# One decode step of cached attention with a token mixer: the query projection laid out by shifted slices of x, and the place of the last output-weight load

## The chip, the core and the metric

The kernel runs on one core of one Trainium2 chip. A core has five engines that run side by side: TensorE (PE, matrix multiplications; its weight loads are shown as PEld), VectorE (DVE), ScalarE (ACT), GpSimd (POOL) and SyncE (SP). Here SP issues all large transfers from main memory (HBM) into on-chip memory (SBUF, 128 partitions), on one queue that 16 DMA engines work through. Matrix products land in PSUM, in banks of 128 partitions x 512 fp32. The metric is the device time of one execution in microseconds (us), as the median of several executions.

## What is computed

One token attends over a cache of 65536 positions with 16 query heads and 8 key/value heads (two query heads share one of them), head size 256. Beside it a small token-mixing MLP works on the same x, and a gate mixes the two. The reference, cut:

```python
B, Sq, D = 1, 1, 448
Hq, Hkv, Sk, Dh = 16, 8, 65536, 256
...
q = (x @ wq).reshape(B, Sq, Hq, Dh).transpose(0, 2, 1, 3)
k = jnp.repeat(k_cache, rep, axis=1)
v = jnp.repeat(v_cache, rep, axis=1)
scores = jnp.einsum("bhqd,bhkd->bhqk", q, k) * (Dh ** -0.5)
p = _softmax(scores, axis=-1)
o = jnp.einsum("bhqk,bhkd->bhqd", p, v)
a = o.transpose(0, 2, 1, 3).reshape(B, Sq, Hq * Dh) @ wo
...
h = _layernorm(x)
u = _gelu(jnp.einsum("bsd,sf->bdf", h, w1) + b1)
b = (jnp.einsum("bdf,fs->bds", u, w2) + b2).transpose(0, 2, 1)
...
g = _sigmoid((x * gate_w).sum(-1, keepdims=True))
return g * a + (1 - g) * b
```

Everything is bf16. The K and V caches are 268 MB each, wq and wo 3.7 MB each.

## The kernel before

Engines are ordered by semaphores written out by hand; no scheduler moves anything. In the setup a small recorder, `do` (lines 41 to 91), adds the waits that follow from the names of what each step reads and writes. Afterwards semaphores are waited on one by one (`take` waits for a semaphore and takes the count off again).

**Chunks.** Each of the 8 KV heads is cut into 6 chunks (`SIZES`, two of 6 and four of 5 blocks of 16 x 128 positions), 48 chunks in all. K of a chunk goes to `kbuf[i % 2]` and V to the single `vbuf`; both hold 6.3 MB. Per chunk:

- DVE (`turns`, L559) turns each K block in 32x32 blocks of fp32 pairs into one of three `kT` tiles.
- PE (`scores`, L685) multiplies `kT` with the window `qw`, which holds the current head pair's queries, into the PSUM bank `sc`. ACT (L632) takes the exponential into `p_t`, DVE turns it (L605), and PE (`p_v`, L699) multiplies it with V of that chunk into `pv`, one chunk later.
- DVE adds `pv` to `og` (`drain_pv`, L569 and L570) and raises `s_vf`: `vbuf` is free.

At the end of a head, DVE forms the next head's window (`queries`, L504), PE turns `og` upright (`o_turn`, L709), DVE divides (`heads`, L577, after `take(dve, s_wo, 16)`), and four matmuls with that head pair's output weights `wo` (L755) add to `acc` and raise `s_oo`: `wo` is free.

**SP's order.** wq (into `vbuf`, which V 0 needs later), K 0, K 1; then SP waits for the projection; V 0, `wo` 0, K 2; then for each i V i (`load_v`, waits for `s_vf` at i + 1), at the second chunk of a head the head's `wo` (`load_wo`, waits for `s_oo`), and K i + 2 (`load_k`). The last V goes in four pieces into the free `kbuf[0]` (L534). The last head's `wo` is issued behind them in two halves with semaphores of their own (L535 to L542).

**The projection** (`project`, L436). x is 448 long. `turn_x` lays it out in columns of 128 partitions (`xT`, 5 columns: three of 128 values, and two for the last 64 values, spread over even and odd partitions). For each of 8 head pairs n, four matmuls (x as the stationary side with one column, 512 columns of wq as the moving side) give one row of 512 values, on partition 32a of `sc` (n = 0 to 3) or `pv` (n = 4 to 7), with `tile_position` choosing column group a. DVE copies both banks (L457), PE turns the rows upright with 32 matmuls of one column (`turn_q`, L466), DVE copies (`qT`, L480), PE spreads `qT` to blocks of 32 partitions with 16 matmuls against an identity (`spread`, L488), DVE copies the result to `qr` (L498). `queries` (L504) multiplies columns of `qr` with a block mask into `qw`.

**The tail** (L762 to L853). With the last V pieces landing, PE multiplies piece by piece (`upright`, L795, then `turned`, L806), DVE divides (L577), PE multiplies with the two halves of `wo` (L840, each half behind its own wait), DVE copies `acc4` to `res` (L847), and SP stores it. POOL waits for the store.

```python
        sp.wait_ge(s_oo, HKV - 1)
        s_wl = [nc.alloc_semaphore(f"s_wl{r}") for r in range(2)]
        for r in range(2):
            at = (HKV - 1) * 512 + r * DH
            sp.dma_start(
                out=wo[:, r, :, :].rearrange("p c n -> p (c n)"),
                in_=A_wo[at:at + DH, :].rearrange("(p c) n -> p (c n)", c=2),
            ).then_inc(s_wl[r], 16)
```

Of the kernel before, what the change touches and what calls it, by code (L numbers as in the profile page):

```python
# [9 lines left out]
BF16 = mybir.dt.bfloat16  # L10
# [4 lines left out]
HQ = 16  # L15
# [79 lines left out]
def kernel(  # L95
# [49 lines left out]
    zb = const.tile([1, 2], FP32, name="zb")  # L145
    ident = const.tile([128, 128], BF16, name="ident")
    block = const.tile([128, 4], FP32, name="block")
# [7 lines left out]
    xd = const.tile([1, 2, 128], BF16, name="xd")  # L155
    xT = const.tile([128, KA + 2], BF16, name="xT")
    xg = const.tile([1, D], FP32, name="xg")
# [11 lines left out]
    h_bc = const.tile([128, D], FP32, name="h_bc")  # L169
    qT = const.tile([128, 2, HQ], BF16, name="qT")  # L170
    qr = const.tile([128, 8, HQ], BF16, name="qr")
    qw = const.tile([128, 8, WIN], BF16, name="qw")
# [8 lines left out]
    tick = const.tile([1, 1], FP32, name="tick")  # L181
    q_row = const.tile([128, 2, 512], BF16, name="q_row")
    oT = const.tile([128, 4], BF16, name="oT")
# [24 lines left out]
    def critical():  # L208
# [55 lines left out]
        for k, src in enumerate((B_w1[0, :], B_b1, B_w2[:, 0])):  # L264
# [7 lines left out]
                out=ident[:], in_=ident[:], compare_op=ALU.not_equal, fill=1.0, base=0,  # L272
                pattern=[[-1, 128]], channel_multiplier=1,
            ), reads=["ident"], writes=["ident"],
# [8 lines left out]
        for t, key, val in (  # L283
            (one_b, "one_b", 1.0), (xd, "xd", 0.0), (one_f, "one_f", 1.0), (zero_b, "zero_b", 0.0),
            (pat, "pat", 0.0), (qw, "qw", 0.0), (col_f, "col_f", 1.0), (pv, "pv", 0.0), (sc, "sc", 0.0),
        ):
            do("dve", lambda e: e.memset(t[:], val), writes=[key])
# [23 lines left out]
        do("pe", turn_x, reads=["x_row", "xd", "one_b"], writes=["x_ps"])  # L311
        do("dve", lambda e: e.tensor_copy(out=xT[:], in_=x_ps), reads=["x_ps"], writes=["xT"])

# [86 lines left out]
        def turn_w(e):  # L400
            for k in range(3):
                last = e.matmul(
                    w_ps[:, k * NF:(k + 1) * NF], lhsT=wrow[:, k, :], rhs=ident[0:NF, 0:NF],
                    start=(k == 0), stop=(k == 2), skip_group_check=True,
                )
            return last
# [26 lines left out]

        q_rows = (sc, pv)

        def project(e):  # L436
            for n in range(8):
                half, a = divmod(n, 4)
                dst = q_rows[half][32 * a:32 * a + 1, :]
                for k in range(KA):  # L440
                    e.matmul(
                        dst, lhsT=xT[:, k:k + 1], rhs=wqa[:, k, n * 512:(n + 1) * 512],
                        start=(k == 0), stop=False, tile_position=(0, 32 * a),
                    )
                last = e.matmul(
                    dst, lhsT=xT[:, KA + half:KA + half + 1], rhs=wqb[:, a * 512:(a + 1) * 512],
                    start=False, stop=True, tile_position=(0, 32 * a),
                )
            return last

        do("pe", project, reads=["wqa", "wqb", "xT", "pv", "sc"], writes=["q_rows"])
        do.need("sp", writes=["wqa", "wqb"])
        load_v(0)
        load_wo(0)
        for half in range(2):
            do(
                "dve", lambda e: e.tensor_copy(out=q_row[0:97, half, :], in_=q_rows[half][0:97, :]),  # L457
                reads=["q_rows"], writes=[f"q_row{half}"],
            )
        q_ps = misc[:, 448:448 + 2 * HQ]  # L460

        def turn_q(e, a):
            for h in (2 * a, 2 * a + 1, 2 * a + 8, 2 * a + 9):
                src = q_row[32 * a:32 * a + 1, h // 8, h % 2 * DH:(h % 2 + 1) * DH]
                for c in range(2):
                    last = e.matmul(  # L466
                        q_ps[:, c * HQ + h:c * HQ + h + 1], lhsT=src[:, c::2],
                        rhs=one_b[32 * a:32 * a + 1, 0:1], start=(h == 0 and c == 0),
                        stop=(h == HQ - 1 and c == 1), tile_position=(32 * a, 0),
                        skip_group_check=True,  # L470
                    )
            return last

        for a in range(4):
            do(
                "pe", lambda e: turn_q(e, a), reads=["q_row0", "q_row1", "one_b", "x_ps"],
                writes=["q_ps", "x_ps"],
            )
        do(
            "dve", lambda e: e.tensor_copy(out=qT[:].rearrange("p c h -> p (c h)"), in_=q_ps),  # L480
            reads=["q_ps"], writes=["qT"],
        )
        qr_ps = misc[:, 0:8 * HQ]

        def spread(e):
            for b in range(4):
                for a in range(4):
                    last = e.matmul(  # L488
                        qr_ps[32 * a:32 * a + 32, b * 2 * HQ:(b + 1) * 2 * HQ],
                        lhsT=ident[:, 32 * b:32 * b + 32], rhs=qT[:].rearrange("p c h -> p (c h)"),  # L490
                        start=(b == 0), stop=(b == 3), tile_position=(0, 32 * a),
                        skip_group_check=True,
                    )
            return last

        do("pe", spread, reads=["ident", "qT", "q_ps"], writes=["qr_ps", "q_ps"])
        do(
            "dve", lambda e: e.tensor_copy(out=qr[:].rearrange("p b h -> p (b h)"), in_=qr_ps),  # L498
            reads=["qr_ps"], writes=["qr"],
        )  # L500

        def queries(h, r):
            cols = slice(PAD + 16 * r, PAD + 16 * r + 97, 32)
            return dve.tensor_tensor(  # L504
                out=qw[:, :, cols], in0=qr[:, :, bass.ds(h, 1)].to_broadcast([128, 8, 4]),
                in1=block[:].rearrange("p (o a) -> p o a", o=1).to_broadcast([128, 8, 4]),
                op=ALU.mult,
            )

        for r in range(2):  # L510
            do("dve", lambda e: queries(r, r), reads=["qr", "block"], writes=["qw"])
        do(
# [7 lines left out]
        for i in range(1, total - 1):  # L520
            load_v(i)
            if i % PER == 1 and PER < i < total - PER:
                load_wo(i // PER)
            if i + 2 < total:
                load_k(i + 2)
# [6 lines left out]
        for k in range(len(edges) - 1):  # L532
            lo, hi = edges[k] * DH, edges[k + 1] * DH
            sp.dma_start(out=vlast[:, lo:hi], in_=src[:, lo:hi]).then_inc(s_last[k], 16)  # L534
        sp.wait_ge(s_oo, HKV - 1)  # L535
        s_wl = [nc.alloc_semaphore(f"s_wl{r}") for r in range(2)]
        for r in range(2):
            at = (HKV - 1) * 512 + r * DH
            sp.dma_start(
                out=wo[:, r, :, :].rearrange("p c n -> p (c n)"),  # L540
                in_=A_wo[at:at + DH, :].rearrange("(p c) n -> p (c n)", c=2),
            ).then_inc(s_wl[r], 16)  # L542

# [47 lines left out]
        def dve_chunk(i, head):  # L591
# [14 lines left out]
            if c == PER - 1 and i < total - 1:  # L606
                for r in range(2):
                    queries(head + r, r)
                den_rows()
                dve.tensor_scalar(  # L610
                    out=og[:], in0=og[:], scalar1=dsum[:, 0:1], scalar2=None, op0=ALU.add
                ).then_inc(s_d, 1)
# [8 lines left out]
        with nc.Fori(0, HKV - 1, 1, engines=[DVE], head_slot={DVE: 0}) as turn_v:  # L621
            for i in range(1, PER + 1):
                dve_chunk(i, turn_v * 2 + 2)
        for i in range(total - PER + 1, total):
# [92 lines left out]

        do.need("pe", reads=["qw", "pv", "mask", "acc", "xb_ps", "w_ps", "qr_ps"])
        do.need("pe", writes=["qr_ps", "w_ps", "xb_ps"])
        c_reg = pe.alloc_register("c_reg")  # L720
# [109 lines left out]
        pe.wait_ge(s_last[3], 16)  # L830
        turned(edges[3], edges[4]).then_inc(s_fp, 1)
        dve.wait_ge(s_fp, 4)
        heads().then_inc(s_fd, 1)
        pe.wait_ge(s_fd, 4)
        for k in range(4):
            r, cc = divmod(k, 2)
            if cc == 0:
                pe.wait_ge(s_wl[r], 16)
            for a in range(4):
                ins = pe.matmul(  # L840
                    acc4[32 * a:32 * a + 1, 0:DQ], lhsT=oT[:, 2 * cc + r:2 * cc + r + 1],
                    rhs=wo[:, r, cc, DQ * a:DQ * (a + 1)], start=False, stop=(k == 3),
                    tile_position=(0, 32 * a), skip_group_check=True,
                )
# [7 lines left out]
        ).then_inc(s_out, 16)  # L852
        pool.wait_ge(s_out, 16)  # L853

# [32 lines left out]
```

## Time and profile before

| what | value |
|---|---|
| runs shown | 1266.63, 1266.64, 1266.64, 1267.09 us |
| median of them | 1266.64 us |
| the profiled execution, its own time | 1266.44 us |
| its span (first to last recorded work) | 1264.7 us |
| mean granted TensorE clock | 0.79 of full |
| read from HBM | 544.22 MB, 430 GB/s over the span |

The profile is of one execution. Busy times are sums over the span; a group of instructions is one source line on one engine, with its count and the mean duration of one. Of the groups, these touch the change (line, work, count, total busy us, mean ns):

```profile
L685 PE MATMUL sc<-kT,qw 128*128 128x512 bf16 x2048 | 565.3, 438 | 454.9 <-PEq L681 454.9
L605 DVE STREAM_TRANSPOSE pT<-p_t 128x512 bf16<-128x512 bf16 x48 | 34.2, 712 | 117.6 <-DVEq L551 117.6
L755 PE MATMUL acc<-wo,oT 128*1 128x448 bf16 x28 | 7.5, 399 | 12.7 <-PEq L752 12.7
```

Behind the second bar stands the idle time of the engine just before such work, and what ended most of it (PEq and DVEq are the engines' own sequencers, which wait for semaphores). An arrow `out<-in` names tiles, and `x` a count. The table of transfers gives for each kind the bytes of one and the median time from issue to landing, which includes the time behind other transfers in the queue.

### The profile page before, as it was taken

To read this page: it belongs to the slowest core of one execution; us is meant where nothing else is said; L and a number is where in the kernel's file an instruction comes from. 1 tells how busy PE (TensorE), PEld (TensorE's weight loads), DVE (VectorE), ACT (ScalarE), POOL (GpSimd) and SP (SyncE) were. 2 spreads that over 40 slices of the span, in tenths; PEclk is the share of its full clock that TensorE was granted. 3 is DMA by queue.
4 is the path that set the end of the run, shared out by engine and by line. 5 is a ranking of instruction groups with operands and counts; after the bars stand their busy time and mean duration, and the time that the engine had idled before them with its cause. 6 is when DMAs were issued, how large, how long until landed. Compare 5 with 4: busy or idle time off the path is not lost. (4 is left out here: it accounts for less than half of the span.)

```text
span 1264.7 us, 10796 instructions
## 1 busy us (share of the span) xinstructions
PE 720.3 (57%) x4344; PEld 282.1 (22%) x4344; DVE 665.5 (53%) x473; ACT 50.1 (4%) x127; POOL 76.7 (6%) x98
## 2 busy tenths in 40 slices
PE   2845656466554655556555565555645665467546
PEld 1311222122211222222222221222212222122212
DVE  4745554465544645455545554465445644466444
ACT  0000000000000000000000000000000000000000
POOL 0001010110110101101111011000000000000000
PEclk9887877868887787777877778778877778777887
DMA  9999999999999999999999999999999999999998
GB/s 411 418 439 429 438 438 425 438 434 429 438 438 427 429 443 427 438 434 433 437 433 427 432 431 443 435 432 431 434 430 439 433 424 435 441 429 439 433 430 343
DMA packets 16844, 544.35 MB, mean 430 GB/s; under 512 B 1856, under 2 KB 3906, under 8 KB 4162
## 3 DMA queue, kind: packets, MB, share of 16 engines
q1 hardware_dynamic: 16744, 544.22, 99.6%
q8 instruction: 4, 0.07, 0.0%
q14 instruction: 6, 0.05, 0.0%
q10 hardware_dynamic: 90, 0.01, 0.0%
HBM read 544.22 MB, written 0.00 MB: 430 GB/s over the span
## 5 line engine op out<-in xcount | busy, mean ns | idle before, releaser
L685 PE MATMUL sc<-kT,qw 128*128 128x512 bf16 x2048 | 565.3, 438 | 454.9 <-PEq L681 454.9
L559 DVE STREAM_TRANSPOSE kT<-kbuf 128x2048 f32<-128x2048 f32 x256 | 571.4, 2284 | 308.2 <-DVEq L551 307.8
L685 PEld LDWEIGHTS sc<-kT,qw 128*128 128x128 bf16 x2048 | 213.9, 108 | 805.5 <-issue 642.6
L699 PE MATMUL pv<-vbuf,pT 128*4 128x512 bf16 x2008 | 132.0, 416 | 56.3 <-PEq L733 55.8
L605 DVE STREAM_TRANSPOSE pT<-p_t 128x512 bf16<-128x512 bf16 x48 | 34.2, 712 | 117.6 <-DVEq L551 117.6
L570 DVE TENSOR_TENSOR og<-pv,og 128x512 f32<-128x512 f32 x39 | 27.0, 692 | 111.5 <-DVEq L551 109.7
L699 PEld LDWEIGHTS pv<-vbuf,pT 128*4 128x4 bf16 x2008 | 51.2, 92 | 134.8 <-issue 96.0
L632 ACT ACTIVATE p_t<-sc 128x512 bf16<-128x512 f32 x48 | 28.7, 597 | 1191.3 <-PE sc L685 1191.3
L659 POOL TENSOR_SCALAR t_b<-t_b 128x448 f32<-128x448 f32 x14 | 7.9, 564 | 358.2 <-ACT t_b L641 358.2
L663 POOL TENSOR_SCALAR t_b<-t_b,hw 128x448 f32<-128x448 f32 x14 | 8.9, 638 | 335.1 <-ACT t_b L649 335.1
L569 DVE COPY og<-pv 128x512 f32<-128x512 f32 x8 | 5.5, 692 | 37.7 <-DVEq L551 37.7
L668 POOL TENSOR_TENSOR ymix<-ymix,t_b 128x448 f32<-128x448 f32 x14 | 16.1, 1148 | 1.1
L667 POOL TENSOR_TENSOR t_b<-t_b,u_b 128x448 f32<-128x448 f32 x14 | 15.8, 1127 | 1.2
L662 POOL TENSOR_TENSOR t_b<-t_b,u_b 128x448 f32<-128x448 f32 x14 | 15.8, 1126 | 1.2
L755 PE MATMUL acc<-wo,oT 128*1 128x448 bf16 x28 | 7.5, 399 | 12.7 <-PEq L752 12.7
L641 ACT ACTIVATE t_b<-h_bc,b1T,w1T 128x448 f32<-128x448 f32 x14 | 10.5, 748 | 0.0
L655 POOL TENSOR_SCALAR u_b<-h_bc,w1T,b1T 128x448 f32<-128x448 f32 x14 | 10.0, 714 | 4.1 <-DVE pat L426 2.7
L632 ACT ACTIVATION_READ_ACCUMULATOR p_t<-sc 128x1 f32 x48 | 9.3, 194 | 0.0
L709 PEld LDWEIGHTS misc<-mask,og 128*128 128x128 f32 x64 | 8.7, 196 | 2.3 <-DVE og L570 1.3
L709 PE MATMUL misc<-mask,og 128*128 128x2 f32 (+1 forms) x64 | 8.0, 249 | 0.8 <-DVE og L570 0.8
L649 ACT ACTIVATE t_b<-t_b 128x448 f32<-128x448 f32 x14 | 7.9, 566 | 0.0
L755 PEld LDWEIGHTS acc<-wo,oT 128*1 128x1 bf16 x28 | 2.0, 85 | 14.6 <-issue 13.2
(98 smaller groups left out, 56.0 us busy)
## 6 DMA issues: line engine op xcount, KB each, us to landing
kbuf<-in_A_k_cache_dram SPq DMA_DIRECT2D x32, 5120.0 KB, 33.0
vbuf<-in_A_v_cache_dram SPq DMA_DIRECT2D x31, 5120.0 KB, 20.8
kbuf<-in_A_k_cache_dram SPq DMA_DIRECT2D x16, 6144.0 KB, 36.1
vbuf<-in_A_v_cache_dram SPq DMA_DIRECT2D x16, 6144.0 KB, 24.6
wo<-in_A_wo_dram SPq DMA_DIRECT2D x7, 448.0 KB, 22.3
vbuf<-in_A_wq_dram SPq DMA_DIRECT2D x1, 3072.0 KB, 10.3
kbuf<-in_A_v_cache_dram SPq DMA_DIRECT2D x1, 2560.0 KB, 26.5
kbuf<-in_A_v_cache_dram SPq DMA_DIRECT2D x1, 1280.0 KB, 31.0
```

Of the source, the lines that this page charges most:

```text
L559: dve.transpose(out=kT[b][:].bitcast(FP32), in_=kn[:, s * SB * 128:(s + 1) * SB * 128]).then_inc(s_kt, 1)
L570: return dve.tensor_tensor(out=og[:], in0=pv[:], in1=og[:], op=ALU.add)
L605: dve.transpose(out=pT[:], in_=p_t[:]).then_inc(s_pt, 1)
L632: ins = act.activation(out=p_t[:], in_=sc[:], func=ACT.Exp, scale=scale, accum_out=den[:, c:c + 1])
L641: ins = act.activation(out=t_b[:], in_=h_bc[:], func=ACT.Square, scale=w1T[:, b:b + 1], bias=b1T[:, b:b + 1],)
L655: lambda: pool.tensor_scalar(out=u_b[:], in0=h_bc[:], scalar1=w1T[:, b:b + 1], scalar2=b1T[:, b:b + 1], op0=ALU.mult, op1=ALU.add,),
L662: lambda: pool.tensor_tensor(out=t_b[:], in0=t_b[:], in1=u_b[:], op=ALU.mult),
L667: lambda: pool.tensor_tensor(out=t_b[:], in0=t_b[:], in1=u_b[:], op=ALU.mult),
L668: lambda: pool.tensor_tensor(out=ymix[:], in0=ymix[:], in1=t_b[:], op=ALU.add),
L685: ins = pe.matmul(sc[:], lhsT=qw[:, q, at:at + 128], rhs=kv[:, :, q // 2, :, q % 2], start=(first and q == 0), stop=(last and q == 7), ski ...
L699: ins = pe.matmul(pv[32 * a:32 * a + 4, :], lhsT=pT[:, k, :, ROW0 + s], rhs=vt[:, j * DH:(j + 2) * DH], start=first and k < 4, stop=last a ...
L709: ins = pe.matmul(o_ps[:, cc, 0:width if half == 0 else 2], lhsT=og[:, half * DH + cc:(half + 1) * DH:2], rhs=mask[:, m:m + (width if half ...
```

## The change

Two things are changed, and a few follow from them.

*The projection.* `xT` becomes `xw`: each of the 5 columns of x is laid at four places, 32 apart, in a row of zeros 135 wide. The slice of 128 columns that starts at 7 - n has x in columns n, 32 + n, 64 + n and 96 + n, and zeros elsewhere. With it as the stationary side, one matmul of full width puts head pair n's row on partition n of each block of 32 partitions, and adds zero to the others. All 32 matmuls accumulate in `sc`. DVE copies the bank once, with the values of a row reordered, and turns it in 32x32 blocks (L466 of the changed kernel) into `qr`. `turn_q`, `spread`, `qT` and their copies go, `ident` shrinks to 14x14, `sc` is no longer cleared, and `queries` takes the head pair n and the row r in place of the head.

*The last `wo`.* The condition that left it out of the loop goes, so the eighth `load_wo` is issued at chunk 43, between V 43 and K 45, as one transfer. The two halves at the end of the queue go with their semaphores. DVE takes `s_wo` in the tail before the last division, PE's waits for the halves go, and the four products come in another order. The wait for the store passes from POOL to SP.

```diff
-    ident = const.tile([128, 128], BF16, name="ident")
+    ident = const.tile([NF, NF], BF16, name="ident")
-    xT = const.tile([128, KA + 2], BF16, name="xT")
+    xw = const.tile([128, KA + 2, 128 + HKV - 1], BF16, name="xw")
-    qT = const.tile([128, 2, HQ], BF16, name="qT")
-    qr = const.tile([128, 8, HQ], BF16, name="qr")
+    qr = const.tile([128, 2, 8, 32], BF16, name="qr")
-    q_row = const.tile([128, 2, 512], BF16, name="q_row")
+    q_row = const.tile([128, 512], BF16, name="q_row")
...
-            (pat, "pat", 0.0), (qw, "qw", 0.0), (col_f, "col_f", 1.0), (pv, "pv", 0.0), (sc, "sc", 0.0),
+            (xw, "xw", 0.0), (pat, "pat", 0.0), (qw, "qw", 0.0), (col_f, "col_f", 1.0), (pv, "pv", 0.0),
...
-        do("dve", lambda e: e.tensor_copy(out=xT[:], in_=x_ps), reads=["x_ps"], writes=["xT"])
+        do(
+            "dve", lambda e: e.tensor_copy(
+                out=xw[:, :, HKV - 1:HKV + 96:32],
+                in_=x_ps.rearrange("p (k o) -> p k o", o=1).to_broadcast([128, KA + 2, 4]),
+            ), reads=["x_ps"], writes=["xw"],
+        )
...
-        q_rows = (sc, pv)
+        q_ps = sc
 
         def project(e):
-            for n in range(8):
-                half, a = divmod(n, 4)
-                dst = q_rows[half][32 * a:32 * a + 1, :]
-                for k in range(KA):
-                    e.matmul(
-                        dst, lhsT=xT[:, k:k + 1], rhs=wqa[:, k, n * 512:(n + 1) * 512],
-                        start=(k == 0), stop=False, tile_position=(0, 32 * a),
+            for n in range(HKV):
+                half, at = divmod(n, 4)
+                for k in range(KA + 1):
+                    if k < KA:
+                        rhs = wqa[:, k, n * 512:(n + 1) * 512]
+                    else:
+                        k, rhs = KA + half, wqb[:, at * 512:(at + 1) * 512]
+                    last = e.matmul(
+                        q_ps[:], lhsT=xw[:, k, HKV - 1 - n:HKV - 1 - n + 128], rhs=rhs,
+                        start=(n == 0 and k == 0), stop=(n == HKV - 1 and k >= KA),
+                        skip_group_check=True,
                     )
-                last = e.matmul(
-                    dst, lhsT=xT[:, KA + half:KA + half + 1], rhs=wqb[:, a * 512:(a + 1) * 512],
-                    start=False, stop=True, tile_position=(0, 32 * a),
-                )
             return last
...
-        for half in range(2):
-            do(
-                "dve", lambda e: e.tensor_copy(out=q_row[0:97, half, :], in_=q_rows[half][0:97, :]),
-                reads=["q_rows"], writes=[f"q_row{half}"],
-            )
-        q_ps = misc[:, 448:448 + 2 * HQ]
-
-        def turn_q(e, a):
...
-        def spread(e):
...
+        do(
+            "dve", lambda e: e.tensor_copy(
+                out=q_row[:].rearrange("p (m c y) -> p m y c", c=2, y=32),
+                in_=q_ps[:].rearrange("p (m y c) -> p m y c", c=2, y=32),
+            ), reads=["q_ps"], writes=["q_row"],
+        )
+        do(
+            "dve", lambda e: e.transpose(
+                out=qr[:].rearrange("p r q n -> p (r q n)"), in_=q_row[:]
+            ), reads=["q_row"], writes=["qr"],
+        )
+
+        def queries(n, r):
             cols = slice(PAD + 16 * r, PAD + 16 * r + 97, 32)
             return dve.tensor_tensor(
-                out=qw[:, :, cols], in0=qr[:, :, bass.ds(h, 1)].to_broadcast([128, 8, 4]),
+                out=qw[:, :, cols], in0=qr[:, r, :, bass.ds(n, 1)].to_broadcast([128, 8, 4]),
...
-            if i % PER == 1 and PER < i < total - PER:
+            if i % PER == 1 and i > PER:
                 load_wo(i // PER)
...
-        sp.wait_ge(s_oo, HKV - 1)
-        s_wl = [nc.alloc_semaphore(f"s_wl{r}") for r in range(2)]
-        for r in range(2):
-            at = (HKV - 1) * 512 + r * DH
-            sp.dma_start(
...
-                    queries(head + r, r)
+                    queries(head, r)
...
-        do.need("pe", reads=["qw", "pv", "mask", "acc", "xb_ps", "w_ps", "qr_ps"])
-        do.need("pe", writes=["qr_ps", "w_ps", "xb_ps"])
+        do.need("pe", reads=["qw", "pv", "mask", "acc", "xb_ps", "w_ps", "q_ps"])
+        do.need("pe", writes=["q_ps", "x_ps", "w_ps", "xb_ps"])
...
+        take(dve, s_wo, 16)
         dve.wait_ge(s_fp, 4)
         heads().then_inc(s_fd, 1)
         pe.wait_ge(s_fd, 4)
         for k in range(4):
-            r, cc = divmod(k, 2)
-            if cc == 0:
-                pe.wait_ge(s_wl[r], 16)
+            cc, r = divmod(k, 2)
             for a in range(4):
                 ins = pe.matmul(
-                    acc4[32 * a:32 * a + 1, 0:DQ], lhsT=oT[:, 2 * cc + r:2 * cc + r + 1],
+                    acc4[32 * a:32 * a + 1, 0:DQ], lhsT=oT[:, k:k + 1],
...
-        pool.wait_ge(s_out, 16)
+        sp.wait_ge(s_out, 16)
```

More of the change, by code (lines that the diff above doesn't have):

```diff
@@ L272, in critical @@
                 out=ident[:], in_=ident[:], compare_op=ALU.not_equal, fill=1.0, base=0,
-                pattern=[[-1, 128]], channel_multiplier=1,
+                pattern=[[-1, NF]], channel_multiplier=1,
             ), reads=["ident"], writes=["ident"],
@@ L402, in turn_w @@
                 last = e.matmul(
-                    w_ps[:, k * NF:(k + 1) * NF], lhsT=wrow[:, k, :], rhs=ident[0:NF, 0:NF],
+                    w_ps[:, k * NF:(k + 1) * NF], lhsT=wrow[:, k, :], rhs=ident[:],
                     start=(k == 0), stop=(k == 2), skip_group_check=True,
@@ L431, in critical @@
         )
-        q_rows = (sc, pv)
+        q_ps = sc
         def project(e):
-            for n in range(8):
-                half, a = divmod(n, 4)
-                dst = q_rows[half][32 * a:32 * a + 1, :]
-                for k in range(KA):
-                    e.matmul(
-                        dst, lhsT=xT[:, k:k + 1], rhs=wqa[:, k, n * 512:(n + 1) * 512],
-                        start=(k == 0), stop=False, tile_position=(0, 32 * a),
-                    )
-                last = e.matmul(
-                    dst, lhsT=xT[:, KA + half:KA + half + 1], rhs=wqb[:, a * 512:(a + 1) * 512],
-                    start=False, stop=True, tile_position=(0, 32 * a),
-                )
+            for n in range(HKV):
[9 more added lines that the diff above has]
+                        skip_group_check=True,
+                    )
             return last
-        do("pe", project, reads=["wqa", "wqb", "xT", "pv", "sc"], writes=["q_rows"])
+        do("pe", project, reads=["wqa", "wqb", "xw"], writes=["q_ps"])
         do.need("sp", writes=["wqa", "wqb"])
@@ L454, in critical @@
         load_wo(0)
-        for half in range(2):
-            do(
-                "dve", lambda e: e.tensor_copy(out=q_row[0:97, half, :], in_=q_rows[half][0:97, :]),
-                reads=["q_rows"], writes=[f"q_row{half}"],
-            )
-        q_ps = misc[:, 448:448 + 2 * HQ]
-        def turn_q(e, a):
[L463 to L478, printed above, removed]
-        do(
-            "dve", lambda e: e.tensor_copy(out=qT[:].rearrange("p c h -> p (c h)"), in_=q_ps),
-            reads=["q_ps"], writes=["qT"],
-        )
-        qr_ps = misc[:, 0:8 * HQ]
-        def spread(e):
[L486 to L494, printed above, removed]
@@ L496, in critical @@
-        do("pe", spread, reads=["ident", "qT", "q_ps"], writes=["qr_ps", "q_ps"])
-        do(
-            "dve", lambda e: e.tensor_copy(out=qr[:].rearrange("p b h -> p (b h)"), in_=qr_ps),
-            reads=["qr_ps"], writes=["qr"],
+        do(
+            "dve", lambda e: e.tensor_copy(
+                out=q_row[:].rearrange("p (m c y) -> p m y c", c=2, y=32),
+                in_=q_ps[:].rearrange("p (m y c) -> p m y c", c=2, y=32),
+            ), reads=["q_ps"], writes=["q_row"],
+        )
@@ L500, in critical @@
+        do(
+            "dve", lambda e: e.transpose(
+                out=qr[:].rearrange("p r q n -> p (r q n)"), in_=q_row[:]
+            ), reads=["q_row"], writes=["qr"],
         )
-        def queries(h, r):
+        def queries(n, r):
             cols = slice(PAD + 16 * r, PAD + 16 * r + 97, 32)
             return dve.tensor_tensor(
-                out=qw[:, :, cols], in0=qr[:, :, bass.ds(h, 1)].to_broadcast([128, 8, 4]),
+                out=qw[:, :, cols], in0=qr[:, r, :, bass.ds(n, 1)].to_broadcast([128, 8, 4]),
@@ L510, in critical @@
         for r in range(2):
-            do("dve", lambda e: queries(r, r), reads=["qr", "block"], writes=["qw"])
+            do("dve", lambda e: queries(0, r), reads=["qr", "block"], writes=["qw"])
         do(
@@ L534, in critical @@
             sp.dma_start(out=vlast[:, lo:hi], in_=src[:, lo:hi]).then_inc(s_last[k], 16)
-        sp.wait_ge(s_oo, HKV - 1)
-        s_wl = [nc.alloc_semaphore(f"s_wl{r}") for r in range(2)]
-        for r in range(2):
-            at = (HKV - 1) * 512 + r * DH
-            sp.dma_start(
-                out=wo[:, r, :, :].rearrange("p c n -> p (c n)"),
-                in_=A_wo[at:at + DH, :].rearrange("(p c) n -> p (c n)", c=2),
-            ).then_inc(s_wl[r], 16)
         plan = [(0, 1), (1, 2), (2, 0), (3, 1), (5, 2), (4, 0)]
@@ L622, in critical @@
             for i in range(1, PER + 1):
-                dve_chunk(i, turn_v * 2 + 2)
+                dve_chunk(i, turn_v + 1)
         for i in range(total - PER + 1, total):
```

## The prediction

> **What bounds the kernel now.** First the totals, then the transfer queue's own table, then the chain of waits, then short windows at the end and the timelines of head and tail. The totals and the queues:
>
> ```profile
> PE 720.3 (57%) x4344; PEld 282.1 (22%) x4344; DVE 665.5 (53%) x473; ACT 50.1 (4%) x127; POOL 76.7 (6%) x98
> ...
> DMA  9999999999999999999999999999999999999998
> ...
> q1 hardware_dynamic: 16744, 544.22, 99.6%
> ```
>
> No engine is busy over 57% of the span, but the packets of the one queue that SP feeds take 99.6% of 16 DMA engines' time over a span of 1264.7 us. That is 1259.6 us, and the first packet starts about 2 us in while the last transfers land about 1261, so the engines have no gap left anywhere between. The bound is the queue: time = start + bytes at the engines' rate + what follows the last landing. The packet records of the trace say how rigid that rate is: nearly all of the 8064 packets of 40960 bytes took 1514 ns. An edit on PE, DVE, POOL or SP can therefore only matter by emptying the queue, by lengthening what follows the last landing, or by changing which bytes land last.
>
> The end, in the chain of waits (start, duration, work):
>
> ```profile
> 1228.48 31.04 DMA kbuf<-in_A_v_cache_dram
> 1259.52 0.05 issue
> 1259.56 1.41 PE misc L806 x48
> 1260.97 0.02 issue
> 1260.99 0.17 DVE oT L577
> 1261.17 0.04 issue
> 1261.21 0.43 PE acc L840 x16
> 1261.64 0.02 issue
> 1261.66 0.27 DVE res L847
> ```
>
> The reader should see that the last release by a transfer is the third of the four last V pieces (1259.52), and that the output weights `wo` are not in the chain, although they are queued behind V. Their issues, with the median from issue to landing:
>
> ```profile
> wo<-in_A_wo_dram SPq DMA_DIRECT2D x2, 224.0 KB, 31.3
> kbuf<-in_A_v_cache_dram SPq DMA_DIRECT2D x1, 256.0 KB, 31.2
> ```
>
> In the timeline SP issues the four V pieces from 1227.53 (0.48 us apart) and the two `wo` halves at 1229.43 and 1229.91. So the fourth V piece lands at 1228.96 + 31.2 = 1260.2 and the `wo` halves at 1260.7 and 1261.2, the last one just as L840 starts at 1261.21. The load of `wo` is covered exactly by the 1.7 us of L806 and L577.
>
> **The change, part by part.**
>
> *The last `wo` moves from the end of the queue to chunk 43.* The issue loop now calls `load_wo(7)` between `load_v(43)` and `load_k(45)`. The same 458,752 bytes are read, but all later K and V stand behind them. By bytes this is 458,752 over the 432 GB/s of the windowed view from 0 to 1259.5, that is 1.06 us. By the packet records it is 256 packets of 1792 bytes at 74 ns, 16 on each engine, 1.18 us. I take 1.18, the records of this very transfer; 1.06 is the lower bound. Each engine works through its share in order, so the last V piece lands where the last `wo` half landed: all four V pieces come 1.18 us later, and L806, L577, L840, L847 and the output follow at their old durations. Term: +1.18 (1.06 to 1.18).
>
> The waits on this path: `load_wo(7)` waits for `s_oo` at 7, raised by the last L755 matmul, which starts at 1128.3; `load_v(43)` ahead of it on SP is issued only at 1153.59. It is met 25 us early. Its issue costs SP 0.43 us (row of L253) and delays `load_k(45)` by that, while the engines have the earlier K and V 43 in hand (V lands 20.8 us after issue, 12 us of them its own transfer). Term 0; if SP's 0.43 were uncovered it would be +0.43. DVE's new `take` of `s_wo` stands before the wait for L806; `wo` lands near 1176 (1153.6 plus about 22 us, the row of L253), 85 us before DVE gets there. Term 0. The removed wait before L840 had been met when its turn came: 0, at most a gain of 0.05 (gap before L840).
>
> *The projection.* Before, 32 matmuls with one-column weights, in four column groups. After, 32 matmuls with 128 columns of `xw`, one bank, one after another.
>
> ```profile
> 13.09 1.48 PE L441 MATMUL sc<-vbuf,xT 128*1 128x512 bf16 x12
> 14.32 0.68 PE L445 MATMUL sc<-vbuf,xT 128*1 128x512 bf16 x4
> 14.75 1.53 PE L441 MATMUL pv<-vbuf,xT 128*1 128x512 bf16 x12
> ...
> 16.85 0.33 SPq L248 DMA_DIRECT2D vbuf<-in_A_v_cache_dram  x1
> ...
> 22.52 0.62 DVE L504 TENSOR_TENSOR qw<-qr,block 128x32 bf16<-128x32 bf16 x2
> 28.07 13.43 DVE L559 STREAM_TRANSPOSE kT<-kbuf 128x2048 f32<-128x2048 f32 x6 [4.92 <-DVEq L551]
> ```
>
> Sixteen matmuls start within 1.66 us, 104 ns apart, so four run at once. The nearest row for whole-array ones is L685: from 30.5 to 36.0, after an idle stretch, its 13 matmuls start 0.427 us apart, and 0.215 later (34 weight loads in 7.29 us), though the windows from 12 to 40 us print a granted clock of 1.00; I go by the spacing. So the 32 take 13 x 0.427 + 19 x 0.215 = 9.6 us, at worst 32 x 0.427 = 13.7, in place of 3.6: they end at 22.7, at worst 26.8. The Trainium skill speaks against this edit in "TensorEngine Tiling (Array Packing)", Key Properties: column tiles work independently and in parallel, and the trace agrees (104 ns). Its "TensorE: Matmul & The Clock Gate", Part 1, has the array at half rate for the first 3.4 us of work only; by that an estimate of 8 slow matmuls and 24 fast ones is 8.6 us, but the row here shows 5.5 us of slow ones, and the row decides.
>
> Behind it: one copy of `q_ps` (the old copies of 97x512 took 0.65 and 0.67; its swapped order may cost up to twice that, so 0.65 to 1.3), one transpose of 128x512 in bf16 (0.71, row of L605), two `queries` (0.62), some 0.2 of gaps. Removed are the second copy, 32 turning matmuls (1.65), 16 spreading ones (0.30) and two casts (0.19, 0.29). `qw` is ready at 22.7 + 2.2 = 24.9, at worst 26.8 + 2.8 = 29.6, against 23.1 now. DVE's next work, the transposes of chunk 0, waits for K until 28.07. So 0, at worst 1.5 late. Late next would be the issue of K 2 (42.07), then V 1:
>
> ```profile
> 42.07 0.34 SPq L242 DMA_DIRECT2D kbuf<-in_A_k_cache_dram  x1
> ...
> 61.19 0.33 SPq L248 DMA_DIRECT2D vbuf<-in_A_v_cache_dram  x1
> ...
> 70.56 6.70 DVE L559 STREAM_TRANSPOSE kT<-kbuf 128x2048 f32<-128x2048 f32 x3 [5.07 <-DVEq L551]
> ```
>
> K 2 lands at about 70.5, so when V 1 is issued the queue still holds 9.3 us of work. V 0's issue waits for the projection and slips from 16.85 to 22.8, at worst 26.9, but K 1 occupies the engines until about 42.5 (K 0's landing plus 6.29 MB at 432 GB/s, 14.5 us). Term 0 (0 to 0). Without that cover it would be the whole 6 to 10 us.
>
> *Small ones.* On DVE, clearing `xw` (675 elements, 0.60 by the `qw` clearing of 1096 in 0.97) replaces clearing `sc` (0.48): +0.12 before the x chain, which then waits for `b2_row` until 11.09. The smaller `ident`, the copy into `xw` and the other strides in `queries` (14 times, on an engine idle 47%) are covered likewise: 0. The wait for the output passes from POOL to SP: hops between engines at the start take 0.5 to 0.7, so -0.6 to +0.6, and 0 as taken, since both engines wait on the same semaphore.
>
> Sum: 0 + 1.18 + 0 = +1.18; span 1264.7 to 1265.9, its own time 1266.44 to 1267.6. The median of the runs is 0.20 above that execution, so the forecast is 1266.64 + 1.18 = 1267.8 us: slower by 0.09%, inside the 0.2% (2.5 us) that I count as what a measurement of this kernel can tell from no change.
>
> **Rivals.** (a) *The old tail was no full load.* Windows near the end show the engines running out unevenly:
>
> ```profile
> 1258.00:1259.00 1.00, 0.99 (x8) 0.91 (x8) 0.00 (x0) 0.00 (x0) 0.00 (x0) 1.00 0.81 304
> 1259.00:1260.00 1.00, 0.44 (x17) 0.44 (x18) 0.00 (x0) 0.00 (x0) 0.00 (x0) 1.00 0.24 90
> ```
>
> If `wo` only filled idle engines there, V's last landing need not move, and the time stays at 1266.6. Against it: the slowest engine has its own sixteenth of `wo`, wherever it stands. (b) *The head starves the queue*: serial projection, late `qw`, late V 1. It decides once `qw` comes 9.3 us after 28.07, at 37.4; each microsecond beyond is a gap of one. Even 32 matmuls at their full 632 ns from start to end (row of L441) would end at 33.3 and give `qw` at 36.1. For +0.2% `qw` must come at 38.8, 1.35 us of gap beside the 1.18; with 2.8 us of gap the time is 1266.64 + 1.18 + 2.8 = 1270.6. (c) *The shorter program end wins*: SP's own wait saves the hop of 0.6, `wo` costs its low 1.06: 1267.1, and less only if the tail shrinks too. That the queue order isn't what the text says is excluded by the built order, where SP's `wo` stands before K 45.
>
> **How the numbers follow.** Forecast 0.72, (a) 0.12, (b) 0.08, (c) 0.08. (a) and (c) lie within 0.2%; beyond it to the fast side nothing has a price, I leave 0.03 of (a) and (c) for it, and 0.03 of the forecast for an unseen slower one. Faster 0.03, same 0.86, slower 0.11. The range runs from (a) less a part of the hop, 1266.4, to the forecast with +0.6 and +0.43 and a little of the runs' own spread of 0.46: 1268.9. The forecast alone: 1267.2 to 1268.4.
>
> **What would show it.** The chain of waits ends with the same lines, each about 1.2 us later, with V's landing first and no `wo`; eight `wo` issues from one line; the queue's total unchanged; the projection at 9 to 14 us with V 0's issue right behind; first transposes within 1.5 us of 28.07. It is wrong if the queue's share falls, if the projection ends after 33, or if the first transposes start after 37.

## The result: 1.35 us slower, and the profile after

| | before | changed |
|---|---|---|
| median, us | 1266.73 (1266.43 to 1267.09, 60 runs) | 1268.08 (1267.85 to 1268.34, 40 runs) |
| profiled execution, us | 1266.44 | 1268.09 |
| its span, us | 1264.7 | 1266.3 |

The ratio is 1.0011, with a 95% interval from 1.0006 to 1.0015: slower by 0.11%, less than the 0.2% that the prediction counted as a change. The forecast was 1267.8 us in a range from 1266.4 to 1268.9.

The queue's table of the changed kernel, the share of DMA engines in 40 slices and the totals of the one queue (packets, MB, share of 16 engines' span):

```profile
DMA  9999999999999999999999999999999999999997
...
q1 hardware_dynamic: 16728, 544.22, 99.5%
```

The bytes are the same and the engines are as full as before; only the last slice is a tenth emptier. The 16 packets fewer are small ones, under 512 bytes; each load brings 16 of them (experiment 6 has seven loads and 112 such packets more), and one load is no longer cut in two. The packet records also give the end of the queue itself: its last packet of data ends at 1260.94 us before and at 1261.08 after. So the queue got hardly longer and has no gap in the middle; what changed is which bytes land last.

The chain of waits of the changed kernel at its end (start, duration, work):

```profile
1229.88 30.89 DMA kbuf<-in_A_v_cache_dram
1260.77 0.05 issue
1260.82 1.42 PE misc L767 x48
1262.24 0.02 issue
1262.26 0.17 DVE oT L538
1262.43 0.04 issue
1262.48 0.57 PE acc L800 x16
1263.05 0.02 issue
1263.07 0.28 DVE res L807
```

It is the chain of before under new line numbers (L806 is L767, L577 is L538, L840 is L800, L847 is L807). The third V piece lands at 1260.77 in place of 1259.52, 1.25 us later; the steps behind it keep their durations but for the last matmuls, 0.57 in place of 0.43. The transfer table of the changed kernel shows why V is late:

```profile
wo<-in_A_wo_dram SPq DMA_DIRECT2D x8, 448.0 KB, 22.2
...
kbuf<-in_A_v_cache_dram SPq DMA_DIRECT2D x1, 256.0 KB, 31.0
```

Eight loads of `wo` now have one kind and one size; none stands behind the last V piece. The fourth V piece still lands while PE works on L767 (by the semaphore records at 1261.40); after it nothing is left to land.

The head, in the timeline of the changed kernel (start, duration, engine, line, work, and the idle time before it):

```profile
12.96 8.65 PE L448 MATMUL sc<-vbuf,xw 128*128 128x512 bf16 x32
...
21.65 2.42 DVE L460 CAST q_row<-sc 128x512 bf16<-128x512 f32 x1 [3.11 <-PE sc L448]
21.70 0.33 SPq L247 DMA_DIRECT2D vbuf<-in_A_v_cache_dram  x1
...
24.11 0.71 DVE L466 STREAM_TRANSPOSE qr<-q_row 128x512 bf16<-128x512 bf16 x1
24.86 0.63 DVE L473 TENSOR_TENSOR qw<-qr,block 128x32 bf16<-128x32 bf16 x2
27.04 4.50 DVE L520 STREAM_TRANSPOSE kT<-kbuf 128x2048 f32<-128x2048 f32 x2 [1.56 <-DVEq L512]
```

The projection takes 8.65 us in place of 3.6, and the queries are ready at 25.5 in place of 23.1. DVE then still waits 1.56 us for K 0, so the lateness ends there.

### The profile page after: what moved, and what is told of

The parts are those of the page before. It is cut to its first block, busy times and chain, and to the rows that moved or that the text cites. A ratio compares the mean times of both kernels' runs of the same rounds, so it can differ in the third digit from the quotient of the medians.

```text
span 1266.3 us, 10696 instructions
## 1 busy us (share of the span) xinstructions
PE 722.9 (57%) x4296; PEld 283.1 (22%) x4296; DVE 667.2 (53%) x471; ACT 50.2 (4%) x127; POOL 76.7 (6%) x98
## 3 DMA queue, kind: packets, MB, share of 16 engines
q1 hardware_dynamic: 16728, 544.22, 99.5%
## 5 line engine op out<-in xcount | busy, mean ns | idle before, releaser
L448 PE MATMUL sc<-vbuf,xw 128*128 128x512 bf16 x32 | 8.7, 438 | 0.0
```

## The experiments

Three parts of the change could carry the 1.35 us: the place of the last `wo` load, the head, and the engine that waits for the store. Each was undone or done alone, the first was multiplied, and the cover of the head was spent until it gave out.

**1. The last `wo` put back.** In the changed kernel:

```diff
-            if i % PER == 1 and i > PER:
+            if i % PER == 1 and PER < i < total - PER:
...
+        sp.wait_ge(s_oo, HKV - 1)
+        s_wl = [nc.alloc_semaphore(f"s_wl{r}") for r in range(2)]
+        for r in range(2):
...
+            ).then_inc(s_wl[r], 16)
...
-        take(dve, s_wo, 16)
...
+            if cc == 0:
+                pe.wait_ge(s_wl[r], 16)
```

> The changed kernel with only the last output weights put back behind V, in two halves with PE's waits for them. My theory: the whole difference of 1.35 us is the place of this load, so the time is that of the kernel before, 1266.7 us, the third V piece lands near 1259.6 on the span's clock, and the output weights are again out of the chain of waits. Rival: the difference comes from the head (serial projection, slower copy) or from the end of the program on SP; then the time stays at 1268.0 to 1268.1.

Measured: 1266.90 us (1266.85 to 1267.05; ratio to before 1.0002, 0.9993 to 1.0011). The line of its chain that answers to the first one above:

```profile
1228.88 30.66 DMA kbuf<-in_A_v_cache_dram
```

That lands at 1259.54, 1.23 us before the changed kernel's. Of the 1.35 us, 1.18 go with this load; 0.17 stay, with SP still waiting for the store (experiments 3 and 4).

**2. The last `wo` moved alone.** The reverse edit, made in the kernel before.

> The kernel before with only the last output weights moved to chunk 43 (DVE's take and the order of the four products go with it). My theory: 1268.0 us, the third V piece lands 1.2 to 1.3 us later than in the kernel before. Rival (head or program end makes the difference): 1266.7 us.

Measured: 1267.93 us (1267.52 to 1268.07; ratio 1.0009, 1.0000 to 1.0018), 1.20 above the kernel before. Its third V piece:

```profile
1229.62 31.01 DMA kbuf<-in_A_v_cache_dram
```

It lands at 1260.63, 1.11 us later than before, with the old head in place. The two runs agree: the load's place is worth 1.2 us, and the head isn't needed for it. (DVE's `take` and the order of the products move with the load in both runs, but the landing itself moves, and they come behind it.)

**3. The store awaited by POOL again.** In the changed kernel:

```diff
-        sp.wait_ge(s_out, 16)
+        pool.wait_ge(s_out, 16)
```

> The changed kernel with the wait for the output store on POOL again. From the issue of the store to the end of the span it was 2.74 us before and 2.92 us after. If SP's wait makes that 0.18 us, this run shows 2.74 and 1267.9 us; if it is scatter, some value between 2.7 and 2.95 and 1268.1 us. My theory: scatter, 1268.1.

Measured: 1267.83 us (1267.62 to 1267.92), 0.25 below the changed kernel; the intervals of the two ratios (1.0000 to 1.0018 and 1.0006 to 1.0015) overlap, so the times alone settle nothing. The profile of this run does better. Its page begins with the span, and its timeline ends with the issue of the store:

```profile
span 1266.0 us, 10696 instructions
```

```profile
1263.36 0.66 SPq L810 DMA_DIRECT2D out_dram<-res  x1
```

From the issue to the end are 1266.0 - 1263.36 = 2.64 us. The same two lines of the changed kernel:

```profile
span 1266.3 us, 10696 instructions
```

```profile
1263.38 0.66 SPq L810 DMA_DIRECT2D out_dram<-res  x1
```

Here it is 2.92. My expectation, scatter, did not hold, and the next run asks again.

**4. SP's wait alone**, the reverse edit in the kernel before.

> The kernel before with only the wait for the output store moved from POOL to SP. In the profiles so far the stretch from the issue of the store to the end of the span is 2.64 to 2.74 us with POOL waiting (three kernels) and 2.91 to 3.01 with SP (six kernels). My theory now, after the run with POOL's wait put back was 0.25 us faster: SP's wait costs 0.2 to 0.3 us, so 1266.95 us and a stretch of 2.9 to 3.0. Rival, scatter between programs: 1266.73 us and 2.7.

Measured: 1266.96 us (1266.83 to 1267.34; before on the same chip 1266.78), and a stretch of 1265.1 - 1262.13 = 2.97, from its span and this line:

```profile
1262.13 0.67 SPq L850 DMA_DIRECT2D out_dram<-res  x1
```

In all eleven profiles POOL's wait gives 2.64 to 2.74 us (4 kernels) and SP's 2.91 to 3.01 (7 kernels), without overlap. The medians moved by 0.18 and 0.25 the same way, though a ratio of 1.0002 (0.9993 to 1.0011) doesn't resolve that by itself. So SP's wait costs 0.2 to 0.3 us in the profiles. The semaphore records of the traces hold the store's landing too, and say it more sharply: from the landing to the end of the span it is 1.04 us in all four kernels with POOL's wait, and 1.29 in six of the seven with SP's (1.34 in experiment 6, where SP has one wait more). The records behind the landing show the difference. At the end of the critical section (L815 of the changed kernel) SP signals the other engines, each of them reports back, and SP collects the reports. With POOL's wait all engines but POOL have done this before the store lands; with SP's wait none has. From the landing to the end of this round it is 0.26 us in the kernel before and 0.49 in this run.

**5. The head alone**: the changed projection, with the old tail and POOL's wait.

> Only the projection part of the change: its head, with the last output weights behind V and POOL waiting for the store, both as in the kernel before. My theory: the head costs nothing, as the projection's 5 us more and the 2.4 us copy end before K 0 lands; 1266.7 us. Rival, that the head costs or gains something that the other two parts have hidden so far: 1266.3 or less, or 1267.1 or more.

Measured: 1266.77 us, beside 1266.78 for the kernel before on the same chip (ratio 1.0000, 0.9991 to 1.0009). The head costs nothing that can be seen. It is also the best version that the parts allow, and it is the equal of the kernel before, not better.

**6. More `wo` in the queue.** Seven loads are issued twice, the copy into a spare tile (the computation is not changed; SP also waits for the copies at the end of the program):

```diff
             if g >= 1:
+                if g >= 2:
+                    sp.wait_ge(s_w2, 16 * (g - 1))
+                sp.dma_start(
+                    out=wo2[:].rearrange("p r c n -> p r (c n)"),
...
+                ).then_inc(s_w2, 16)
                 sp.wait_ge(s_oo, g)
```

> The changed kernel with seven of its eight output-weight loads issued twice, the copy into a tile of its own, so 3.21 MB more in the queue. By the packet records (16 packets of 74 ns on each engine for one load, 1.18 us) it is 8.3 us slower: 1276.4 us. By bytes at 432 GB/s (1.06 us a load): 1275.5. Rival, that the queue has room in which such a load hides: less than 1270.

Measured: 1276.08 us (1276.04 to 1276.14; ratio 1.0074, 1.0059 to 1.0089), 8.00 above the changed kernel, 1.14 us a load. The queue's totals in its page:

```profile
q1 hardware_dynamic: 18632, 547.43, 99.5%
```

3.21 MB more at the same share: nothing hides in this queue, and a load ahead of the last V costs its own transfer time. The price lies between my two bounds (1.06 by bytes, 1.18 by packets).

**7. The projection computed twice**, to make the head late on purpose:

```diff
-            for n in range(HKV):
+            for n in [*range(HKV)] * 2:
```

> The changed kernel with its projection computed twice (64 matmuls, the second round starts its sums anew). The second round runs at the full rate, 32 x 0.216 = 6.9 us, so the queries are ready at 25.5 + 6.9 = 32.4 us, 5.4 us after the first transposes started in the changed kernel (27.04). My theory, that the queue's backlog hides lateness up to about 11 us (the 9.3 of the prediction, and 1.9 in which PE waited for V 0): no change, 1268.1 us. Rival, that lateness of the head goes to the end: 1273.5 us.

Measured: 1268.76 us, with a wide spread (1268.08 to 1269.44; ratio 1.0015, 1.0006 to 1.0025); the profiled execution took 1268.11. In its timeline:

```profile
65.33 0.33 SPq L247 DMA_DIRECT2D vbuf<-in_A_v_cache_dram  x1
...
70.50 8.89 DVE L520 STREAM_TRANSPOSE kT<-kbuf 128x2048 f32<-128x2048 f32 x4 [0.87 <-DVEq L512]
```

DVE's first transposes start at 33.68, 6.6 us late, V 1 is issued only 4.4 us late (65.33 for 60.95), and K 2 lands as ever, some 70 us in, 5 us after that issue. The queue never ran dry in this execution, and of 6.6 us none reached the end. The other executions did not all do as well: eight of the ten lie above 1268.34 us, the slowest of 40 of the changed kernel, so the 0.7 us by which the median lies higher are more than scatter (the kernel before reads 0.1 us higher on that chip). My expectation of no change holds for the profiled execution and one other; what costs the rest their time no trace shows.

**8. The projection computed four times**, the same edit with 4.

> The changed kernel with its projection computed four times. The queries come 20.7 us later, at 46.2 us, 19.1 us after 27.04; V 0 is issued at 42.4 us, about when K 1 has landed. My theory: V 1 would be issued near 78 us while K 2 has landed at 70.5, so the queue runs dry for some 8 us and the time is 1275 to 1277 us. Rival, that the head is covered without bound: 1268.1. Rival, that all lateness goes to the end: 1287.

Measured: 1280.22 us (1279.59 to 1281.30; ratio 1.0106, 1.0089 to 1.0123), 12.1 above the changed kernel. Windows of its profile (stretch, length, busy time of PE, PEld, DVE, ACT and POOL, granted clock, share of the DMA engines, GB/s):

```profile
40.00:44.00 4.00, 3.80 (x18) 1.45 (x16) 0.44 (x1) 0.00 (x0) 0.00 (x0) 1.00 0.03 12
...
76.00:80.00 4.00, 4.00 (x53) 1.66 (x42) 2.54 (x2) 0.00 (x0) 0.00 (x0) 1.00 0.00 0
```

and three issues in its timeline:

```profile
43.61 0.33 SPq L247 DMA_DIRECT2D vbuf<-in_A_v_cache_dram  x1
...
61.37 0.34 SPq L241 DMA_DIRECT2D kbuf<-in_A_k_cache_dram  x1
...
79.10 0.33 SPq L247 DMA_DIRECT2D vbuf<-in_A_v_cache_dram  x1
```

The queue is dry twice: until V 0, whose issue waits for the projection, and until V 1. In between it runs short a third time, until K 2. (A packet is counted in the window in which it starts; by the packet records no engine works for 2.6 us from 42.0 and for 3.9 from 76.2, around K 2's issue the engines are idle for 1.0 us in the mean, and over the first 100 us this makes 10.4 us in place of 0.4.) I had expected 1275 to 1277, since I counted one gap and left out V 0's, which I had put at the edge of its cover, and K 2's. The mechanism of rival (b) exists: the profile with the first transposes 6.6 us late shows no gap, the one with 20.5 us shows these. The changed kernel's queries were 2.4 us later than before, with 1.56 us to spare.

**9. The copy in another order.** The one copy of the projection had taken 2.42 us, well over its price:

```diff
-                out=q_row[:].rearrange("p (m c y) -> p m y c", c=2, y=32),
-                in_=q_ps[:].rearrange("p (m y c) -> p m y c", c=2, y=32),
+                out=q_row[:].rearrange("p (m c y) -> p m c y", c=2, y=32),
+                in_=q_ps[:].rearrange("p (m y c) -> p m c y", c=2, y=32),
```

> The changed kernel, where the one copy of the projection is made in another order: it writes runs of 32 neighbours and reads every second value, where the changed kernel writes every 32nd. I had priced that copy at 0.65 to 1.3 us and it took 2.42. If the writing order makes it slow, it takes 0.65 to 0.75 here; if the reading order does, it stays at 2.4. The time of the whole stays at 1268.1 either way, as the copy is covered.

Measured in one execution: 1268.11 us, and in its timeline:

```profile
22.66 0.69 DVE L460 CAST q_row<-sc 128x512 bf16<-128x512 f32 x1 [3.99 <-PE sc L448]
```

The same 512 elements take 0.69 us when neighbours are written one after another, 3.5 times less. (The slow order, exactly: each write lies 31 or 32 elements from the one before, back and forth between two runs of 32, and the reads go through the row in order.) So the order in which it writes bf16 made it slow, not the order in which it reads fp32 from PSUM.

## Why the prediction was right, and where a size was off

*The bound.* The step held: the queue's share stayed (99.6%, 99.5%), and experiment 6 shows that 3.21 MB more cost 8.00 us with no room to hide in.

*The term of +1.18.* Right, and shown from both sides: 1.18 taken out, 1.20 put in, 1.14 a load when multiplied. The third V piece landed 1.25, 1.23 and 1.11 us later in three pairs of profiles. Over the runs with no load or projection added it landed at 1259.51 to 1259.71 in the four with the load last and at 1260.63 to 1260.77 in the four with it at chunk 43, 1.15 apart in the mean, so one profiled pair holds it to about 0.2. The waits priced at 0 on this path (`s_oo`, DVE's `take`, PE's waits on the halves) show up in no chain.

*The program end, taken as 0 with bounds from -0.6 to +0.6.* The one term of the sum that was mis-sized: 0.2 to 0.3 us by the profiles, 0.18 and 0.25 by the medians. "0 as taken, since both engines wait on the same semaphore" was the weak reason: what follows the semaphore differs (0.25 us by the traces, experiment 4), and no row of before that the prediction shows bore on that. With it the sum is 1.18 + 0.2 = 1.4, and 1.35 was measured. The other part of the miss is the start value: the forecast is 0.26 us under the measured 1268.08, and 0.09 of that is the median of before, 1266.73 over 60 runs and 1266.64 over the four that I had.

*The last matmuls*, 0.57 for 0.43, belong to no part of the change. Windows of the changed kernel, and of the kernel before (granted clock third from the end):

```profile
1261.00:1262.00 1.00, 1.00 (x44) 1.00 (x42) 0.00 (x0) 0.00 (x0) 0.00 (x0) 1.00 0.00 0
1262.00:1262.50 0.50, 0.24 (x13) 0.16 (x13) 0.16 (x1) 0.00 (x0) 0.00 (x0) 0.55 0.00 0
1262.50:1263.00 0.50, 0.50 (x16) 0.26 (x16) 0.00 (x0) 0.00 (x0) 0.00 (x0) 0.50 0.00 0
```

```profile
1261.00:1261.50 0.50, 0.29 (x16) 0.19 (x16) 0.15 (x1) 0.00 (x0) 0.00 (x0) 0.91 0.00 0
1261.50:1262.00 0.50, 0.12 (x8) 0.00 (x0) 0.27 (x1) 0.00 (x0) 0.00 (x0) 0.50 0.00 0
```

The granted clock falls to 0.50 just ahead of them. In the kernel before it fell while they ran. Of the other profiles, eight show 0.56 or 0.57, with the clock down by 0.05 us after the first of these matmuls at the latest, and one shows 0.40, with the clock down only as they end (experiment 6). Among the eight is the kernel before with only SP's wait moved. The profiled execution of before caught the better side, which can be 0.14 of the 0.29 us by which its 1266.44 lay under the median.

*The head, priced at 0.* Right (experiment 5), with two sizes off inside the cover. The copy took 2.42 us where I allowed 0.65 to 1.3; reading and writing across the row don't cost alike, and I had no row for a strided write. The projection took 8.65 us in this profile where I had 9.6. I had taken 5.5 us of half rate from the row of L685; here the half-rate spacing lasts from 12.95 to 16.27, 3.3 us. In the five other profiles with this same projection it lasts 4.6 to 5.9 us, and the projection takes 9.28 to 9.94, so my 9.6 was the nearer figure in all five. The estimate of 8.6 us from the Trainium skill's "TensorE: Matmul & The Clock Gate", Part 1, is nearer for the profile of the changed kernel alone; against half rate for the first 3.4 us only, the five measured longer. That section also says that the window in which the activity is watched runs freely, so that the count of slow matmuls differs from run to run. In that the runs agree with it.

*The rivals.* (a), no loss because the old tail was not full, is excluded by experiments 1 and 2. (b), a starving head, needs far more lateness than this change makes, but its first gap is V 0's issue, not V 1's alone, and its price was short: queries ready at 47.4, 10.0 us past its point of 37.4, should have cost 10.0, and 12.1 was measured. The engines' added idle time in the first 100 us is 10.0; slower packets after each gap (below) add 2.7, and 0.6 is saved at the end, where the engines run out more evenly. (c) had the sign of the program end wrong.

## What to carry to other kernels

Where one queue is full from end to end, as here, a transfer costs its own time wherever it stands ahead of the data that the last work waits for. Behind those data it is covered for as long as that work lasts: put last what needs the least work behind it. Work ahead of the first transfer that is waited for is free up to a backlog that can be read from the issue and landing times; look for every issue that waits for this work, not only the first consumer. A term that no row bears on belongs into the range, even when it looks like nothing.

## What the runs showed that I had not expected

- A DVE copy of 128x512 from fp32 in PSUM to bf16 took 2.42 us when each write lay 31 or 32 elements from the one before, and 0.69 us when it wrote neighbours and read every second element.
- The wait for the output store on SP ends the program 0.2 to 0.3 us later than on POOL (1.29 us or more from the store's landing against 1.04): the engines' round at the end of the critical section then comes wholly behind the landing.
- DVE starts to turn K 0 at 27.0 to 27.3 us in the six profiles in which V 0 is issued at 21.7 to 23.05, and at 28.06 to 28.15 in the three in which it is issued at 16.4 to 17.0. An issue made early may hold up what is already under way by 1 us, but the three are also the ones with the old projection, so another part of the old head may be the cause; this was not tried by itself.
- When the queue has run dry, it doesn't pick up at its full rate: in the run with the projection computed four times, the packets took 2.7 us more on each engine in the mean (1262.7 for 1259.9), beside the idle time, about 0.8 of it in the 2 us behind each of the three gaps.
